# Clustered attention into a Fourier mix and an FFN on one core: scores from float16 halves for every pair, one turned head in each first-sequence pair, odd weight pieces split on GpSimd

## The chip, the cores and the metric

One core of a Trainium2 chip runs the kernel. The metric is the device time of one execution in microseconds. Three runs of the kernel before took 983.2, 986.29 and 989.46 us, the median being 986.29.

## What is computed

Four sequences of 768 tokens, 8 heads of 64 dimensions. In each head every query and key goes to the nearest of 16 centroids, and a query attends only to keys of its own cluster. The result is mixed by a two-dimensional Fourier transform (its real part), normalised, and goes through an FFN of 512 x 2048 x 512 with two residual additions.

```python
q_assign = np.argmax(np.einsum('bhsd,hcd->bhsc', q_n, c_n), axis=-1)
k_assign = np.argmax(np.einsum('bhsd,hcd->bhsc', k_n, c_n), axis=-1)
mask = q_assign[:, :, :, None] == k_assign[:, :, None, :]
scores = np.where(mask, scale * np.matmul(q, k.transpose(0, 1, 3, 2)), -1000000000.0)
attn = np.exp(scores - np.max(scores, axis=-1, keepdims=True))
attn_out = np.matmul(attn / (np.sum(attn, axis=-1, keepdims=True) + 1e-09), v)
X = np.fft.fft(np.fft.fft(x, axis=1), axis=2)          # x: the heads side by side
u = x + np.real(X)
un = (u - mean) / np.sqrt(var + 1e-06)
out = u + np.maximum(un @ w_ch1, 0.0) @ w_ch2
```

## The kernel before

Everything wants float32 accuracy. Most products are therefore made of float16 halves: a value is scaled by a power of two, split into a high half and the low rest, and three products (high by high, high by low, low by high) are summed in PSUM. Where float32 itself is used, TensorE takes the operands as they are.

Heads are worked in 16 pairs, four for each sequence; a pair's two heads lie in the two halves of the 128 partitions.

- `prep(pr)` loads q and k (`load`), takes the largest magnitudes (`largest`, VectorE), spreads them over the partitions and makes powers of two of them (`scales`), splits q and k (`split_qk`: the high half cast by ScalarE, the low one subtracted by VectorE), multiplies with the centroids, transposes the 16 cluster scores, finds the best cluster and makes one-hot rows, which a transposing DMA turns into `oht`. For pairs below `FULL`, that is 0 to 5, q and k are kept as float32: their magnitudes are not taken, they are not split, and the products with the centroids (line 441) and the scores (line 506) are float32.
- `scores(pr)` has six steps (128 queries each). A step makes the scores of both heads (line 506 or 509) and adds the cluster penalty by one-hot products (line 514); for each head VectorE then takes the row maximum (line 528) and ScalarE the exponential (line 530). For a head that is not in `TURN`, the result is cast to float16 (line 540 on GpSimd for pairs 0 to 3, line 542 on ScalarE for the others), the low half is subtracted on GpSimd (line 543), and both are transposed by a DMA on SP's queue into one of six buffers `pt`.
- `turns(pr)` does this for the heads in `TURN`: TensorE transposes the float32 result (line 562), VectorE or ScalarE copies it out of PSUM (lines 565 and 567).
- `attend(pr)` multiplies with V: 18 float16 products for a transposed head (lines 595 to 597), float32 ones for a turned head (line 590). `finish` divides by the sums (lines 605 to 609) and writes the pair's columns of X.

`Weights` loads the two FFN matrices in 32 pieces of 128 x 512 and splits each into halves: `signs` (ScalarE), `block` (a common scale), `join` (TensorE puts the float32 value into PSUM) and `halve`: ScalarE writes the high half from PSUM, VectorE the low one (lines 734 and 735). `Fourier.transform` runs when a sequence's four pairs are finished; `norms` and `layer` of `FeedForward` follow, with the up-projection at line 1064 and the down-projection at line 1106.

The order is written by hand twice over. `PLAN` is a list of words: `s0*2` means two further steps of pair 0's scores, `w` a step of the weights, `f1` one of the second sequence's FFN, and so on; it sets the order in which instructions are created. `TABLE` then permutes each engine's own list by relative jumps, and `apply` fixes the result by dependencies. Each engine works strictly in its order. Weights, transposes and loads all stand on SP's queue. The buffers around the change: one `scr` for natural q and k, two each of `hlq` and `hlk` for split ones, two of `ph` and two of `p32`, two score tiles in PSUM (`ps_big`), three of `ps_f`, one of `ps_o`.

## Time and profile before

| what | value |
|---|---|
| median of three runs | 986.29 us |
| profiled execution, its time | 981.39 us |
| its span (first to last instruction) | 979.5 us |
| TensorE busy | 924.7 us (94%) |
| VectorE busy | 560.1 us (57%) |
| ScalarE busy | 565.8 us (58%) |
| GpSimd busy | 552.7 us (56%) |
| granted TensorE clock, mean | 0.991 |

Busy time on TensorE runs to the modelled end of each matmul, so neighbours overlap, and a stretch that shows 100% has no visible gap but is not an array at its peak. How long a group really holds TensorE is read from start to start. On VectorE, too, one instruction starts a little before the end of the one ahead. A row of the table of stages gives, after the stretch, the busy microseconds and the count of instructions of each engine, the granted clock as a share of full speed, and the mean share of time that the 16 DMA engines had work (over 1 where transfers queue).

### The profile page before, as it was taken

What the parts mean: (1) busy time and instruction counts of PE and PEld (TensorE: products, weight loads), DVE (VectorE), ACT (ScalarE), POOL (GpSimd) and SP (SyncE); (2) the same over time, 40 slices, a digit from 0 to 9 for tenths busy, and PEclk for the clock granted to TensorE, in tenths of its full rate; (3) what the DMA queues carried; (4) which work ended last, traced back from release to release, by engine and by line L of the source; (5) the groups of instructions that cost most, each with busy time, mean ns of one, the idle gap of its engine ahead of it and who ended that gap; (6) DMA issues with size and microseconds to landing.
All of it is one profiled execution on the core that took longest, in us unless ns stands there. A gap on an engine that the chain in (4) does not pass through costs nothing.

```text
span 979.5 us, 23040 instructions
## 1 busy us (share of the span) xinstructions
PE 924.7 (94%) x9189; PEld 614.9 (63%) x9189; DVE 560.1 (57%) x1314; ACT 565.8 (58%) x896; POOL 552.7 (56%) x675
## 2 busy tenths in 40 slices
PE   3889999788999999999999999999999999999998
PEld 1357658465657657567757658667667585677583
DVE  5887897877556555577656664677544324611010
ACT  5667776567656756567757657368666552433140
POOL 2751640449956757559957758369857552553140
PEclk9999999898999999999999999999999999999999
DMA  9894993497877789497888777587757642311000
GB/s 345 182 236 154 228 254 79 100 186 159 150 139 128 151 148 168 78 176 166 157 174 145 128 153 158 95 168 158 129 99 135 115 76 61 66 33 33 12 12 22
DMA packets 359739, 131.18 MB, mean 134 GB/s; under 512 B 344272, under 2 KB 345296, under 8 KB 359632
## 3 DMA queue, kind: packets, MB, share of 16 engines
q1 hardware_dynamic: 359632, 129.72, 65.1%
q8 instruction: 72, 1.18, 0.5%
q14 instruction: 35, 0.29, 0.1%
HBM read 43.17 MB, written 6.29 MB: 50 GB/s over the span
## 4 chain that ended last, share of the span: by engine, by line
PE 51%; DMA 13%; POOL 6%; ACT 5%; DVE 3%; issue 3%; SPq 1%; POOLq 0%; ACTq 0%; DVEq 0%
PE ps_f L1064 21%; PE ps_f L1106 18%; DMA pt<-ph 11%; POOL ph L543 4%; PE ps_big L509 4%; ACT ph L542 2%; PE ps_o L595 2%; PE ps_f L912 1%; PE ps_o L596 1%; PE ps_o L597 1%; PE ps_big L514 1%; ACT p L530 1%; PE ps_big L506 1%; POOL arena L1073 1%; DVE ps_big L528 1%
## 5 line engine op out<-in xcount | busy, mean ns | idle before, releaser
L543 POOL TENSOR_TENSOR ph<-p,ph 128x768 f16<-128x768 f32 x144 | 240.1, 1671 | 148.5 <-ACT ph L542 141.0
L1064 PE MATMUL ps_f<-arena,w1h 128*128 128x256 f16 x1536 | 266.3, 274 | 7.2 <-DMA arena<-arena 3.3
L1106 PE MATMUL ps_f<-w2h,arena 128*128 128x512 f16 x768 | 237.5, 379 | 0.0
L1064 PE MATMUL ps_f<-arena,w1l 128*128 128x256 f16 x768 | 210.6, 274 | 0.0
L1106 PEld LDWEIGHTS <-arena 128*128 128x128 f16 x1152 | 109.5, 98 | 125.8 <-issue 2.1
L530 ACT ACTIVATE p<-ps_big,rmx 128x768 f32<-128x768 f32 x144 | 128.6, 898 | 76.6 <-DVE ps_big L528 53.0
L528 DVE TENSOR_SCALAR_CACHE_REDUCE ps_big<-ps_big,sce 128x768 f32<-128x768 f32 x120 | 118.6, 1023 | 88.6 <-PE ps_big L514 83.0
L1073 POOL TENSOR_TENSOR arena<-arena 128x256 f16<-128x256 f32 x192 | 129.1, 680 | 70.8 <-ACT arena L1072 66.8
L1064 PEld LDWEIGHTS <-w1h 128*128 128x128 f16 x1536 | 151.0, 98 | 24.9 <-DMA arena<-arena 3.4
L542 ACT CAST ph<-p 128x768 f16<-128x768 f32 x144 | 119.1, 830 | 71.4 <-DMA pt<-ph 70.3
L1106 PE MATMUL ps_f<-w2l,arena 128*128 128x512 f16 x384 | 145.5, 379 | 0.0
L595 PE MATMUL ps_o<-v,pt 128*128 128x66 f16 x1008 | 105.5, 194 | 17.5 <-DMA pt<-ph 16.1
L1072 ACT ACTIVATE arena<-ps_f,wrel 128x256 f16<-128x256 f32 x192 | 89.6, 473 | 43.4 <-DVE arena L1069 43.2
L595 PEld LDWEIGHTS <-pt 128*128 128x128 f16 x1008 | 92.2, 96 | 33.3 <-DMA pt<-ph 20.9
L1069 DVE TENSOR_SCALAR arena<-ps_f,wrel 128x256 f32<-128x256 f32 x96 | 46.2, 481 | 114.4 <-PE ps_f L1064 85.1
L596 PE MATMUL ps_o<-v,pt 128*128 128x64 f16 x1008 | 105.1, 194 | 0.0
L597 PE MATMUL ps_o<-v,pt 128*128 128x66 f16 x1008 | 104.6, 192 | 0.0
L596 PEld LDWEIGHTS <-pt 128*128 128x128 f16 x1008 | 92.9, 97 | 2.9 <-issue 0.3
L597 PEld LDWEIGHTS <-pt 128*128 128x128 f16 x1008 | 93.2, 99 | 0.0
L1064 PEld LDWEIGHTS <-w1l 128*128 128x128 f16 x768 | 75.5, 98 | 13.9 <-issue 4.5
L1071 ACT ACTIVATE arena<-ps_f,wrel 128x256 f32<-128x256 f32 x96 | 45.3, 472 | 46.3 <-PE ps_f L1064 41.3
L509 PE MATMUL ps_big<-hlk,hlq 64*128 64x384 f16 x720 | 70.7, 324 | 1.2 <-ACT p L530 1.1
(196 smaller groups left out, 1379.2 us busy)
## 6 DMA issues: line engine op xcount, KB each, us to landing
arena<-in_moe_w_ch_dram SPq DMA_DIRECT2D x32, 512.0 KB, 5.0
vst<-in_v_dram SPq DMA_DIRECT2D x16, 384.0 KB, 4.1
out_dram<-arena SPq DMA_DIRECT2D x24, 256.0 KB, 2.1
scr<-in_q_dram SPq DMA_DIRECT2D x12, 384.0 KB, 3.9
scr<-in_k_dram SPq DMA_DIRECT2D x12, 384.0 KB, 4.5
pt<-ph SPq DMA_TRANSPOSE x156, 3.9
arena<-in_cs_dram SPq DMA_DIRECT2D x12, 192.0 KB, 4.0
arena<-in_ss_dram SPq DMA_DIRECT2D x12, 192.0 KB, 3.9
```

What stands on the lines that cost most here:

```text
L509: nc.tensor.matmul(out=ps[j][:, hf, 0:SH], lhsT=hq[rows[j], a, sl], rhs=hk[rows[j], c, hs], start=(i == 0), stop=False)
L528: nc.vector.tensor_scalar(out=ju, in0=ps[j][:, :, 0:SH], scalar1=ne, scalar2=None, op0=ALU.mult, op1=ALU.min, accum_out=m)
L530: nc.scalar.activation(x, ju, AF.Exp, bias=m, scale=-1.0)
L542: nc.scalar.copy(out=ph[:, 0], in_=p32)
L543: nc.gpsimd.tensor_tensor(out=ph[:, 1], in0=p32, in1=ph[:, 0], op=ALU.subtract)
L595: nc.tensor.matmul(out=o[:, at:at + W], lhsT=hi, rhs=v16[:, kt, 0:W], start=(kt == 0), stop=False)
L596: nc.tensor.matmul(out=o[:, at:at + D], lhsT=hi, rhs=v16[:, kt, 66:130], start=False, stop=False)
L597: nc.tensor.matmul(out=o[:, at:at + W], lhsT=lo, rhs=v16[:, kt, 0:W], start=False, stop=(kt == ST - 1))
L1064: nc.tensor.matmul(out=ps.rearrange("p (t x) -> p t x", x=P), lhsT=a[:, dc, fs], rhs=c[:, :, dc], start=(i == 0), stop=(i == 11))
L1072: nc.scalar.activation(hh[:, f], ps, AF.Relu, scale=rel[:, f:f + 1])
L1073: nc.gpsimd.tensor_tensor(out=hl[:, f], in0=r, in1=hh[:, f], op=ALU.subtract)
L1106: nc.tensor.matmul(out=ps, lhsT=a[:, f, ts], rhs=c[:, f], start=(i == 0), stop=(i == 47))
```

## The change

Five edits.

1. `FULL` goes from 6 to 0: no pair keeps float32 q and k. Pairs 0 to 5 load into `scr`, take all three magnitudes, split q and k, and use the float16 paths for the centroids and the scores, as pairs 6 to 15 do already.
2. `TURN` names the second head of each of pairs 0 to 3, where it named both heads of pairs 1 and 3. There are four turned heads as before.
3. `halve` treats odd pieces in another way: ScalarE copies the scaled float32 value to SBUF, one buffer at `X32`, and GpSimd subtracts the high half. Even pieces stay as they were.
4. `load` has a condition for small `FULL` that is never true at 0.
5. `PLAN` and `TABLE` are new throughout.

```diff
-2 -3 0 1 .2 6 0 3 0 -13 12 0 -13 12 -13 12 -16 16 -15 4 10 0 -17 4 6 4 1 -17 10 6 2 -7 1 4 0 -5 0 3 8 -9 0 11 -12 .2 4 0 -6 5
+.9 4 -5 .3 3 -3 0 3 -3 0 1 5 -4 -3 0 12 27 -35 -6 0 1 0 3 -3 0 32 0 -33 0 4 -4 0 28 0 -30 4 -4 0 26 0 -28 1 0 24 0 -23 -4 0
...
-    TURN = {(1, 0), (1, 1), (3, 0), (3, 1)}
+    TURN = {(p, 1) for p in range(4)}
     EV = {(st, 0) for st in range(6)}
-    FULL = 6
+    FULL = 0
...
-        if pr < self.FULL and pr % 3:
+        if pr < self.FULL and (pr % 3 or self.FULL < 3):
...
         nc.scalar.activation(hi, ps, AF.Copy, scale=s)
-        nc.vector.scalar_tensor_tensor(out=lo, in0=ps, scalar=s, in1=hi, op0=ALU.mult, op1=ALU.subtract)
+        if k % 2:
+            x = self.arena.at(self.X32 if k < 32 - 2 * self.LATE else self.place(k), [P, DM], F32)
+            nc.scalar.activation(x, ps, AF.Copy, scale=s)
+            nc.gpsimd.tensor_tensor(out=lo, in0=x, in1=hi, op=ALU.subtract)
+        else:
+            nc.vector.scalar_tensor_tensor(out=lo, in0=ps, scalar=s, in1=hi, op0=ALU.mult, op1=ALU.subtract)
...
     PLAN = """
-w v0 p0 v1 c l*2 c p0*2 v2 p1 p2 l*2 v3 p0 v0*2 p1 l w p1 p0*4 w p1 s0*2 a0 s0*7 p1*2 s0*2 p1 a0*2 s0 p1 p3*2 w*3 l w*2 l w
+p0*2 w p0 v0 p0*5 l p1 c*2 p0*2 l*2 w p1*2 l p0*2 l v1 p1*3 p2 p1 w*2 p1 w*3 p1 l v2 w l w*3 p1 l*2 s0*2 u0 s0*2 u0 s0*2 v0
```

What this does to the engines' orders is shown at three places. Line numbers of the changed kernel are one higher up to line 735 and six higher behind line 741; `L415` there is the split that was line 414, `L529` the row maximum that was 528, `L741` the even pieces' low half, `L738` and `L739` the two new instructions of odd pieces.

The first place is VectorE, around the first row maximum of pair 0. Before, it stands behind the one-hot rows of pair 1 (`oh`) and the scale of the first weight block:

```order
L395 TENSOR_REDUCE amx<-vst 128x1
L472 TENSOR_TENSOR oh<-ac,ps_f 128x12x16
L59 TENSOR_SCALAR ps_f<-ps_f 128x1
L476 TENSOR_TENSOR oh<-ac,ps_f 128x6x16
L61 TENSOR_SCALAR winv_85<-ps_f 128x1
L476 TENSOR_TENSOR oh<-ac,ps_f 128x6x16
L63 RECIPROCAL wsc<-winv_85 128x1
L528 TENSOR_SCALAR X_64,rmx<-ps_big 128x768 x2
L735 SCALAR_TENSOR_TENSOR w1l<-ps_f,wsc,w1h 128x512
```

In the changed kernel the scales and the splits of pair 1 stand ahead of it:

```order
L633 TENSOR_SCALAR sce<-scp 128x1 x2
L415 SCALAR_TENSOR_TENSOR hlq<-scr,scp,hlq 128x768
L415 SCALAR_TENSOR_TENSOR hlk<-scr,scp,hlk 128x768
L715 TENSOR_REDUCE arena<-ps_f 128x1
L729 SCALAR_TENSOR_TENSOR ps_f<-arena,ps_f 128x512
L58 TENSOR_SCALAR ps_f<-arena 128x1
L729 SCALAR_TENSOR_TENSOR ps_f<-arena,ps_f 128x512
L59 TENSOR_SCALAR ps_f<-ps_f 128x1
L368 SCALAR_TENSOR_TENSOR v_599<-vst,scp,v_599 128x6x64
L61 TENSOR_SCALAR winv_85<-ps_f 128x1
L63 RECIPROCAL wsc<-winv_85 128x1
L529 TENSOR_SCALAR X_64,rmx<-ps_big,sce 128x768
```

Pair 0's own reductions and splits stand further up, ahead of the centroids; the row maximum now has two heads' worth of preparation ahead of it, and its scale is read from `sce`.

The second place is GpSimd, in the steps of pair 0 and 1, where `p_391`, `p_624` and the like are the second kind of buffer for transposed heads. Before, both heads of a step come together, two casts and two subtractions:

```order
L540 CAST ph<-X_64 128x768
L540 CAST p_264<-X_64 128x768
L543 TENSOR_TENSOR ph<-X_64,ph 128x768
L543 TENSOR_TENSOR p_264<-X_64,p_264 128x768
L540 CAST ph<-X_64 128x768
```

In the changed kernel one head of a step comes at a time, and subtractions of weight pieces stand between them:

```order
L541 CAST p_624<-X_64 128x768
L544 TENSOR_TENSOR p_624<-X_64,p_624 128x768
L739 TENSOR_TENSOR w1l<-arena,w1h 128x512
L541 CAST ph<-X_64 128x768
L544 TENSOR_TENSOR ph<-X_64,ph 128x768
L541 CAST p_771<-X_64 128x768
L544 TENSOR_TENSOR p_771<-X_64,p_771 128x768
L739 TENSOR_TENSOR w1l<-arena,w1h 128x512
```

So a transpose of the first sequence can have a weight piece ahead of it, which none had.

The third place is VectorE, around the last finish of pair 3 (line 609, then 610) and the fold of the Fourier step (line 851, then 857). Before, four low halves of the weights come behind that finish:

```order
L609 TENSOR_TENSOR X_63<-ps_o,rs 128x3x128
L773 TENSOR_TENSOR winv_86<-winv_86,winv_85 128x16
L735 SCALAR_TENSOR_TENSOR w2l<-ps_f,wsc,w2h 128x512 x2
L728 SCALAR_TENSOR_TENSOR ps_f<-arena,ps_f 128x512 x2
L851 TENSOR_TENSOR arena<-X_63 128x1536
L735 SCALAR_TENSOR_TENSOR w2l<-ps_f,wsc,w2h 128x512 x2
L528 TENSOR_SCALAR ps_big,rmx<-ps_big 128x2x384 x2
```

In the changed kernel the weights are through by then, and the splits of pair 5 and reductions of a later pair have their place:

```order
L610 TENSOR_TENSOR X_63<-ps_o,rs 128x3x128
L857 TENSOR_TENSOR arena<-X_63 128x1536
L415 SCALAR_TENSOR_TENSOR hlq<-scr,scp,hlq 128x768
L529 TENSOR_SCALAR ps_big,rmx<-ps_big,sce 128x2x384 x2
L415 SCALAR_TENSOR_TENSOR hlk<-scr,scp,hlk 128x768
L529 TENSOR_SCALAR ps_big,rmx<-ps_big,sce 128x2x384 x2
L841 SCALAR_TENSOR_TENSOR arena<-arena,vseq 128x768
```

What moved here is which foreign work stands between the steps of the first Fourier transform: weights before, preparation of pairs now.

## Rows read from the trace of the kernel before

**Rows 1.** Busy times by stage: stretch, each engine's microseconds (instructions), clock, DMA.
```profile
core 0: us, PE busy (x) PEld busy (x) DVE busy (x) ACT busy (x) POOL busy (x), PEclk, DMA share, GB/s
0.00:30.00 30.00, 13.00 (x55) 5.32 (x55) 17.78 (x64) 15.18 (x21) 8.26 (x45) 1.00 0.80 292
30.00:181.00 151.00, 142.68 (x1317) 94.22 (x1315) 123.19 (x290) 107.42 (x143) 66.05 (x70) 0.99 0.79 182
181.00:229.00 48.00, 35.80 (x381) 23.45 (x379) 40.52 (x96) 28.37 (x45) 30.41 (x30) 0.92 0.93 177
229.00:979.00 750.00, 733.23 (x7440) 491.92 (x7440) 378.59 (x868) 414.81 (x690) 447.96 (x533) 1.00 0.61 115
```
**Rows 2.** Timeline (start, microseconds, instruction): pair 3's last finish, the first up-projection.
```profile
180.58 0.54 DVE L609 TENSOR_TENSOR X<-ps_o,rs 128x384 f32<-128x384 f32 x1
...
229.30 0.39 PE L1064 MATMUL ps_f<-arena,w1h 128*128 128x256 f16 x1 [3.26 <-DMA arena<-arena]
```
**Rows 3.** Busy times in four stretches of the first stage, columns as in rows 1.
```profile
40.00:60.00 20.00, 17.65 (x204) 9.45 (x204) 17.90 (x47) 15.04 (x18) 17.98 (x16) 1.00 1.17 236
75.00:110.00 35.00, 35.00 (x275) 26.58 (x276) 26.40 (x59) 25.38 (x34) 9.89 (x9) 1.00 0.59 168
110.00:145.00 35.00, 32.94 (x359) 19.32 (x358) 31.86 (x80) 26.50 (x35) 21.64 (x25) 0.95 1.14 239
145.00:180.00 35.00, 35.00 (x283) 26.88 (x283) 26.66 (x64) 21.87 (x32) 2.77 (x6) 1.00 0.27 77
```
**Rows 4.** TensorE's timeline: a float32 score step, a float16 one, what follows each.
```profile
61.09 1.56 PE L506 MATMUL ps_big<-hlk,hlq 64*128 64x384 f32 x8
62.59 0.34 PE L514 MATMUL ps_big<-oht 32*128 32x384 bf16 x4
...
401.11 1.15 PE L509 MATMUL ps_big<-hlk,hlq 64*128 64x384 f16 x12
402.19 0.34 PE L514 MATMUL ps_big<-oht 32*128 32x384 bf16 x4
```
**Rows 5.** TensorE's groups by line: count, busy microseconds, mean ns; idle before.
```profile
L446 PE MATMUL ps_f<-hlq,ct 128*32 128x384 f16 x60 | 6.7, 329 | 0.2 <-ACT arena L1072 0.2
...
L441 PE MATMUL ps_f<-hlq,arena 128*32 128x384 f32 x16 | 4.0, 585 | 0.0
```
**Rows 6.** VectorE's groups by line and shape, whole span.
```profile
L395 DVE TENSOR_REDUCE amx<-scr 128x1 f32<-128x768 f32 x20 | 18.8, 946 | 8.8 <-DMA scr<-in_q_dram 8.8
...
L414 DVE SCALAR_TENSOR_TENSOR hlq<-scr,scp,hlq 128x768 f16<-128x768 f32 x10 | 15.2, 1522 | 0.8 <-ACT hlq L413 0.8
...
L735 DVE SCALAR_TENSOR_TENSOR w1l<-ps_f,wsc,w1h 128x512 f16<-128x512 f32 x16 | 11.7, 747 | 1.9 <-ACT w1h L734 1.9
...
L414 DVE SCALAR_TENSOR_TENSOR hlk<-scr,scp,hlk 128x768 f16<-128x768 f32 x10 | 11.0, 1097 | 0.0
...
L405 DVE TENSOR_REDUCE ps_f<-ps_f 128x3 f32<-128x384 f32 x10 | 5.6, 560 | 2.6 <-PE ps_f L48 2.5
...
L405 DVE TENSOR_REDUCE ps_f<-ps_f 128x1 f32<-128x128 f32 x6 | 1.8, 296 | 1.7 <-PE ps_f L48 1.7
```
**Rows 7.** A split of q: shortest, median, longest of ten; one behind a subtraction.
```profile
L414 DVE SCALAR_TENSOR_TENSOR hlq<-scr,scp,hlq x10: 1012/1336/2394, 228.9 to 698.5; 128x768 f16<-128x768 f32 x10
...
322.98 1.65 POOL L543 TENSOR_TENSOR ph<-p,ph 128x768 f16<-128x768 f32 x1
...
323.35 2.09 DVE L414 SCALAR_TENSOR_TENSOR hlq<-scr,scp,hlq 128x768 f16<-128x768 f32 x1
```
**Rows 8.** Groups by line on ScalarE and GpSimd that the added instructions resemble.
```profile
L734 ACT ACTIVATE w1h<-ps_f,wsc 128x512 f16<-128x512 f32 x16 | 10.6, 680 | 8.4 <-DVE wsc L63 8.0 <-DVE ps_f L728 0.3
...
L413 ACT ACTIVATE hlq<-scr,scp 128x768 f16<-128x768 f32 x10 | 9.3, 928 | 5.0 <-DVE scp L630 2.5 <-PE ps_big L506 1.4 <-PE ps_big L509 1.1
...
L1034 POOL TENSOR_TENSOR arena<-arena 128x512 f16<-128x512 f32 x20 | 24.4, 1219 | 8.4 <-ACT arena L1033 8.3
```
**Rows 9.** Busy times in a stretch with a lowered clock, columns as in rows 1.
```profile
185.00:196.00 11.00, 8.09 (x66) 5.23 (x66) 11.00 (x17) 5.16 (x7) 6.43 (x3) 0.69 0.60 126
```

More of the change, by code (lines that the diff above doesn't have):

```diff
@@ L153 @@
[L153 to L156 removed]
+.28 11 3 -16 1 -2 18 2 -21 1 0 -3 7 -6 6 -7 0 3 -4 5 .3 1 0 1 .2 1 0 -3 15 0 -14 0 -3 3 0 -3 4 0 -3 -2 4 0 -3 6 -3 2 .2 48 0
@@ L157 @@
+-26 -9 .3 11 18 2 -3 -29 28 67 -67 -12 11 -30 2 33 -37 -3 2 1 1 1 71 .3 1 -79 1 0 1 -2 1 24 45 30 -102 0 14 -15 1 14 -15 0 65
+4 -71 0 93 .2 -88 88 -89 13 -12 11 -14 1 56 18 0 -3 -73 79 1 -82 51 -52 .2 9 0 -11 10 -11 10 0 -10 9 0 -11 10 -11 10 1 -13 10
+1 -13 12 .6 52 -53 .5 44 -28 -18 17 -18 17 0 -12 11 -12 11 .2 -14 13 -14 13 .5 15 -16 3 8 5 .3 1 -2 1 -8 -3 0 8 0 12 .2 17
+-18 17 -24 -11 0 9 -10 0 12 0 25 -40 13 25 -40 39 -40 0 39 -40 39 0 -41 40 1 -34 .5 26 1 -8 -22 .6 2 .8 11 0 14 -15 .13
 """,
@@ new lines @@
+0 1 -9 8 1 -5 49 0 -49 44 0 -45 .3 -26 2 22 1 .3 1 5 -6 .2 25 -26 -6 5 1 0 10 -10 0 -18 27 7 -19 0 6 -7 .4 4 2 -3 0 -17 11 5
+0 2 4 .3 7 -8 0 11 -12 0 1 23 -26 1 1 .3 2 7 -11 2 10 -11 .2 8 -9 5 -6 7 -8 8 0 1 -2 7 -7 .3 45 -43 0 41 -41 36 0 -38 -8 0 6
+0 -25 0 23 0 13 -12 -3 13 -14 3 1 0 7 -8 0 -8 0 -12 41 -25 3 -4 4 .2 5 -6 0 5 -22 44 -30 0 4 .2 5 7 -8 .6 1 6 -7 0 -24 1 43
+-23 0 38 -29 -11 2 .2 5 -6 5 -6 6 -2 -6 0 7 0 -4 3 1 .4 49 -49 1 .2 2 0 -8 44 0 1 -61 9 15 -11 0 2 0 5 -5 0 30 -31 2 .2 25
@@ L166 @@
+-26 9 -10 .8 1 18 -19 .3 15 -16 .7 8 .9 1 0 -3 2 0 2 -3 2 -3 2 .3
 """,
@@ new lines @@
+p10 t1 v12 s9*4 p10 f0 p10 f0 s9*2 p10 f1*3 s9*2 f1 f0 p10 f1*2 p12*2 t1 p11 p10 p11 a8*5 p11 a8 p10*2 t1 p13 s10*3 f1*6 s10
+f1*3 p11 v9*2 a9*2 f1 v11*2 s10 a9*3 p12 a8 f1 a9 f1 s10 n1 f1 v10 n1 a9*8 n1 p11 f1 n1 s10*6 p12 n1 f1 p11 v10 f1 p14 f1
+p11*2 f1 p12 f1 p14 p12 p11 p12 f1 p12 f1*4 a10 v12 p12 a10*3 p11 s11 a10*6 f1 a10*2 s11*2 f1 t2 v13 a10 a11 p12 a10 a11 s11
+a11*2 f1 p12 s11*3 f1 s11 a11*4 s11 f1 s11*2 p12 s11 f1 a11 s12*3 a11*2 s12*2 a11 f1*6 p13*4 f1 a11 f1 p13 s12*7 a11 f1*4
+p13*3 f1*2 p13 a12 f1*6 v12 f1*6 a12 f1*2 a12 p13 f1*2 p13 f1 p14 t2 a12 t2 f1 s13 f1 t2*2 a12 p15 t2 a12 v13 a12*2 p14 a12*4
@@ new lines @@
+v13 t2*7 v14 a12 s13 t2 p14 t2*2 a12 f1 t2*3 f1 t2*2 p15 p14*2 s13 f1 s13 t2 s13 v14 s13*2 a13*4 t2*2 s13 n2 f2 s13 f2*4 s13
+f2*2 v15 f2*2 p15 p14 p15 v14 p14 f2*4 a13*2 f2 n2 a13*2 s13 f2 p14 a13 s13 a13 p14 p15*2 f2 a13 f2 a13 p14 n2 f2 a13 f2*2
+s14*4 a14 s14 a13 f2*3 s14*2 a14 v15*2 s14*5 p15 f2*6 p15 f2 p15 f2 a14*2 f2 a14 f2*2 p15*2 f2 a14*9 f2 p15 f2*7 s15 a15
+s15*7 n2 s15*4 a15*5 n2 a15*8 t3 f2*24 t3 n2 f2*2 t3*14 f2*2 t3*3 f2 t3 n3*2 t3*2 f3*10 n3*2 f3*21 t3 f3*9 t3 f3*2 n3 f3 n3
+f3*29
```

162 lines of the change are left out of this document (72 added, 90 removed).

## The prediction

> **What bounds the kernel now.** I read the page first, then the busy times by stage, then the timeline around the places the change touches. The program falls into three stages [rows 1]: until 181 us the attention of the first sequence (pairs 0 to 3) beside the conversion of the FFN weights; from 181 to 229 us the Fourier step and the first norm; from 229 us on the FFN with the other sequences beside it. The last finish of pair 3 on VectorE begins at 180.58 us and the first up-projection at 229.30 us [rows 2]. In the third stage TensorE is busy 733.2 of 750 us: what it no longer has to do there comes off the end, and so does whatever moves the 229 us.
>
> The first stage is not TensorE's alone. It alternates [rows 3]. Where a pair has both heads turned by TensorE (75 to 110 us, 145 to 180 us) TensorE is busy 35.0 of 35.0 us, VectorE 26.4 and 26.7, and the DMA share is 0.59 and 0.27. Where a pair has none (40 to 60, 110 to 145) VectorE is busy 17.9 of 20 and 31.9 of 35, nine tenths, the DMA share is 1.17 and 1.14, and TensorE has gaps. So two engines set the pace in turn, and VectorE shows in these rows how densely it can be packed: 0.90. Over the whole of 30 to 181 us it is busy 123.2 of 151, that is 0.82 [rows 1].
>
> **TensorE's work.** A score step of pairs 0 to 5 is 8 float32 records, 1.50 us from its start to that of the one-hot products behind it (61.09 to 62.59); with float16 halves it is 12 records in 1.08 us (401.11 to 402.19) [rows 4]. Six steps in six pairs: 36 x 0.42 = 15.1 us less. The cluster products: one side's float32 rows take 4.0 us in four pairs, the float16 ones 6.7 us in ten [rows 5], so 0.33 x 6 = 2.0 us less. The scales of these pairs take three small products instead of one, 12 more, some tenths of a microsecond each at most, and I take 1 us more. Together 16 us less. The turned heads stay four, so transposes, evictions and float32 products only change their place, and the transposes through DMA stay 24 in the first sequence.
>
> Of these 16 us most lie ahead of 229 us: of the 36 float32 steps 31 stand in TensorE's order ahead of the first up-projection, 5 behind it. In the changed order 32 of the 36 stand ahead. The stage behind 229 us so loses 5 x 1.50 - 4 x 1.08 = 3.2 us, and TensorE being full there, **3 us come off the end**. What the other 13 us bring depends on who sets the 229 us.
>
> **VectorE's work in the first stage**, counted in the two orders up to the second finish of pair 3, with durations from [rows 6]:
> - 9 more reductions for the scales of q and k, 0.946 each: +8.5 us.
> - 10 more splits of q and k (two of pair 5 come later): 5 x (1.522 + 1.097) = +13.1 us.
> - six reductions over three columns instead of one, 0.560 against 0.296: +1.6 us. Twelve one-column multiplies for the score's scale: between nothing and 0.3 each; I take 1.8 us.
> - the low halves of the odd weight pieces leave: 16 subtractions instead of 28 stand ahead of this point, 12 x 0.747 = -9.0 us.
>
> Sum +16 us. Bounds: with splits at their shortest (1.01) and the multiplies at nothing 11 us; with all ten splits at the longest that the rows show for one (2.39) [rows 7] and the multiplies at 3.6, 28.6 us. Nothing below the lower bound is possible, as the reductions and splits are instructions that were not there. VectorE was busy 141.0 us until 181 [rows 1]; it will need about 157, between 152 and 170.
>
> **ScalarE and GpSimd.** ScalarE gets 12 casts of q and k at 0.93 and 16 copies of odd pieces at 0.68 [rows 8]: 22 us on top of the 122.6 us that it is busy until 181 [rows 1], 80% of the time: covered, as long as the stage is not shorter than some 160 us. GpSimd gets 16 subtractions of 128x512. It has no such one of a weight piece before; the nearest row is that of the norm, 1.22 us with the same shapes [rows 8]: 20 us on 74.3 until 181, covered too. What is queued behind them are its casts and subtractions for the next transposes; in the order shown they stand one at a time between those, so a transpose is late by 1.2 us, not more. If that cover went, each would delay a product, and TensorE waits for it.
>
> **The start.** The first softmax of pair 0 stands on VectorE behind the scales and the four splits of pairs 0 and 1: four reductions and four splits, 4 x 0.946 + 2 x 2.62 = 9 us, in a stretch of which VectorE leaves 12 of 30 us idle [rows 1]. I take half of it as hidden: the first scores come some 4 us later, with pair 1 already prepared, and VectorE has then done 22 us of its work at 30 us instead of 17.8. On SP's queue q and k of pair 0 are now first, ahead of V and the weights; their number stays.
>
> **Sum.** The stage ends where VectorE is through: 157 - 22 = 135 us at the 0.90 that rows 3 show it holding, 150 us from 30 us on, so at 180 us instead of 181. TensorE then needs less than its 155.7 us and has room. From there to 229 us VectorE is busy 40.5 of 48 us [rows 1]; three reductions and two splits come in (5.5 us), four weight subtractions leave (3.0 us): the 7.5 us idle hide that; uncovered it would be 2.5. So 1 us, and 3 us behind 229: 4 us less. The profiled execution took 981.4 us with a span of 979.5; the median of the three runs is 986.3, and the sum goes onto that: **982 us**. The likeliest case by itself reaches from 974 (VectorE packed at 0.95) to 990 (0.85).
>
> **Rivals.**
> (1) TensorE still sets the first stage. For it speaks that the four stretches of [rows 3] are full in turn, two on TensorE and two on DMA and VectorE, and that one turned and one transposed head in each pair spreads both loads evenly. VectorE would have to hold 135 us in 138, 0.98, against it. But if the splits cost 1.01 and the start hides all nine microseconds, it is 152 - 27 = 125 us in 138, 0.91, just what it has shown. Then all 16 us come off: 970 us.
> (2) Slower: GpSimd holds VectorE up. A split of q takes 1.01 us at its shortest and 2.39 at its longest; the one at 323.35 us begins while GpSimd's subtraction of 322.98 (1.65 us) runs, and takes 2.09 [rows 7]. The change puts ten such splits and at least 16 GpSimd instructions into the same stage. At 2.39 each VectorE needs 170 us: 148 at 0.90 is 164 us from 30 us on, an end at 194, 13 us late. TensorE, idle for longer, would also lose clock: between 185 and 196 us its granted clock is 0.69, a stretch at the lower of its two levels (1.2 instead of 2.4 GHz) after it had waited, and costs (1 - 0.69) x 11 = 3.4 us [rows 9]. One more of these: 986 + 13 + 3 - 3 = 999 us. From an end of the stage at 194 us on, the kernel is slower by more than 1%. Against it: the splits' mean of 1.3 us already holds such meetings, at a GpSimd that is busier in the third stage (448 of 750) than in the first (66 of 151).
> The Trainium skill, "SBUF — State Buffer", section "SBUF: two separate sides", gives a reason: VectorE and GpSimd share a pair of ports that is locked for a whole instruction, and a VectorE instruction with two SBUF inputs, as the split is, blocks against a GpSimd one that reads SBUF. By that rule, the trace agrees (2.09 us behind a running subtraction against 1.01 alone); by that rule alone moving subtractions from VectorE, where one input is in PSUM, to GpSimd while adding splits is the wrong way round, and would end at the 999 us of this rival.
>
> **Chances.** VectorE-paced with nothing gained or lost in the stage 0.45; TensorE-paced 0.31; VectorE held up or packed badly by the new order 0.24. About 1% is what a measurement of this kernel can tell from no change: 976.4 to 996.2 us. Faster by more: rival 1 and a little of the first case's lower end, 0.33. Slower by more: most of rival 2, 0.22. Within: 0.45. Range: from below rival 1 (967, when the waits on DMA of the two stretches without turned heads go too) to rival 2 (1000).
>
> **What would show it.** The second finish of pair 3 (180.6 us before) and the first up-projection (229.3): at 180 and 228 in my case, near 169 and 216 in rival 1, at 194 and beyond 240 in rival 2. VectorE's share in 34 to 180 us near 0.90, and TensorE's below the 142.7 of 151. A score step of pair 0 at 1.1 us. The splits' mean near 1.3 us; at 2 us rival 2 holds. Behind the first up-projection the rest should take 747 us; if it takes more than 755, the new order of the third stage, which I took as equal to the old one, is what failed.

## The result, and the profile after

The change made the kernel slower. Its median is 996.08 us over nine runs (990.41 to 998.85), against 985.45 us for the kernel before in nine runs beside them: ratio 1.0102, with a 95% interval of 1.0084 to 1.0120. Forecast were 982 us and a gain of 4. The profiled execution of the changed kernel has a span of 991.1 us, 11.6 more than before.

In the changed kernel's code line numbers are one higher than before as far as line 735, six higher behind 741. Its busy times by stage (stretch, each engine's microseconds with instructions, clock, DMA), cut where its own stages end, answer to [rows 1]:

```profile
core 0: us, PE busy (x) PEld busy (x) DVE busy (x) ACT busy (x) POOL busy (x), PEclk, DMA share, GB/s
0.00:30.00 30.00, 8.85 (x38) 3.95 (x38) 18.92 (x60) 17.07 (x23) 6.57 (x42) 1.00 0.69 243
30.00:183.40 153.40, 135.02 (x1435) 93.03 (x1454) 139.07 (x318) 121.27 (x165) 87.14 (x88) 0.98 0.79 188
183.40:239.60 56.20, 36.71 (x471) 24.29 (x471) 46.77 (x99) 35.71 (x54) 36.96 (x36) 0.88 0.87 173
239.60:991.10 751.50, 729.04 (x7408) 489.39 (x7408) 373.54 (x860) 409.33 (x685) 444.36 (x527) 1.00 0.61 114
```

The second stage of the kernel before, cut in the same way, beside it:

```profile
180.60:229.30 48.70, 36.20 (x383) 23.45 (x379) 41.22 (x97) 28.98 (x45) 31.11 (x30) 0.92 0.92 176
```

The two marks of [rows 2], on VectorE's and TensorE's timeline after:

```profile
183.42 0.55 DVE L610 TENSOR_TENSOR X<-ps_o,rs 128x384 f32<-128x384 f32 x1
```
```profile
239.58 0.28 PE L1070 MATMUL ps_f<-arena,w1h 128*128 128x256 f16 x1 [2.13 <-DMA arena<-arena]
```

So the first stage ends 2.8 us later than before, the second takes 56.2 us instead of 48.7 (7.5 more), the third 751.5 instead of 750.2. TensorE is busy 909.6 us instead of 924.7: the 15 us that were to leave it did leave it, and it waits for 27 us more. In the third stage, too, where 3 us were to come off, its busy time falls by 4.2 us and its waits grow by 5.5 (17.0 to 22.5), so that nothing comes off.

The longest stall stands at the start of the second stage. VectorE's timeline there:

```profile
184.00 1.91 DVE L857 TENSOR_TENSOR arena<-X 128x1536 f32<-128x1536 f32 x1
185.84 5.95 DVE L415 SCALAR_TENSOR_TENSOR hlq<-scr,scp,hlq 128x768 f16<-128x768 f32 x1
191.71 1.01 DVE L529 TENSOR_SCALAR_CACHE_REDUCE ps_big<-ps_big,sce 128x768 f32<-128x768 f32 x1
```

and GpSimd's in the same microseconds:

```profile
184.26 2.23 POOL L869 TENSOR_TENSOR arena<-arena,X 1x255 f32<-1x255 f32 x1
186.46 1.63 POOL L544 TENSOR_TENSOR ph<-p,ph 128x768 f16<-128x768 f32 x1
188.06 1.15 POOL L739 TENSOR_TENSOR w2l<-arena,w2h 128x512 f16<-128x512 f32 x1
189.18 1.79 POOL L858 TENSOR_TENSOR arena<-arena 128x765 f32<-128x765 f32 x1
```

One split of q (pair 5, L415) takes 5.95 us; the sixteen of them in the kernel:

```profile
L415 DVE SCALAR_TENSOR_TENSOR hlq<-scr,scp,hlq x16: 1007/1019/5948, 12.8 to 708.7; 128x768 f16<-128x768 f32 x16
```

(shortest, median, longest). GpSimd runs four instructions without a pause from 184.26 to 190.97 us, one of them (L739) new: VectorE's order has no weight piece left behind the finish, but GpSimd's still has this one. The split is through 0.8 us after the run. The row maxima of pair 4 (L529) stand behind it. What TensorE waits for from 181 to 240 us:

```profile
PE ps_big L510 <- ACT p L531: 8.5, 6, 4.6
PE ps_o L596 <- DMA pt<-ph: 5.1, 2, 3.2
PE ps_f L918 <- DMA arena<-arena: 2.3, 2, 1.4
PE ps_f L1070 <- DMA arena<-arena: 2.1, 1, 2.1
```

The first line, waiting for pair 4's exponentials, was 1.1 us in that stretch before:

```profile
PE ps_big L506 <- ACT p L530: 1.1, 2, 0.7
```

The split that holds up their row maxima was my first suspect.

### The profile page after: what moved, and what is told of

The parts are those of the page before. It is cut to its first block, busy times and chain, and to the rows that moved or that the text cites. A ratio compares the mean times of both kernels' runs of the same rounds, so it can differ in the third digit from the quotient of the medians.

```text
span 991.1 us, 23402 instructions
## 1 busy us (share of the span) xinstructions
PE 909.6 (92%) x9350; PEld 610.7 (62%) x9369; DVE 578.3 (58%) x1334; ACT 583.4 (59%) x924; POOL 575.0 (58%) x691
## 4 chain that ended last, share of the span: by engine, by line
PE 45%; DMA 18%; POOL 9%; DVE 8%; ACT 7%; issue 4%; SPq 1%; another core or an unknown queue 0%; POOLq 0%; ACTq 0%; DVEq 0%
PE ps_f L1112 18%; PE ps_f L1070 15%; DMA pt<-ph 14%; POOL ph L544 6%; PE ps_big L510 4%; ACT ph L543 3%; PE ps_f L918 2%; DMA arena<-arena 2%; DVE X L529 1%; ACT p L531 1%; PE ps_o L596 1%; DVE ps_big L529 1%; PE ps_big L515 1%; DVE amx L396 1%; PE ps_o L597 1%
## 5 line engine op out<-in xcount | busy, mean ns | idle before, releaser
L529 DVE TENSOR_SCALAR_CACHE_REDUCE ps_big<-ps_big,sce 128x768 f32<-128x768 f32 x144 | 142.0, 1021 | 77.9 <-PE ps_big L515 66.5
L1079 POOL TENSOR_TENSOR arena<-arena 128x256 f16<-128x256 f32 x192 | 132.4, 696 | 78.4 <-ACT arena L1078 73.9
L510 PE MATMUL ps_big<-hlk,hlq 64*128 64x384 f16 x1152 | 117.0, 328 | 12.6 <-ACT p L531 9.5
L1075 DVE TENSOR_SCALAR arena<-ps_f,wrel 128x256 f32<-128x256 f32 x96 | 46.2, 481 | 119.9 <-PE ps_f L1070 86.7
L510 PEld LDWEIGHTS <-hlq 64*128 64x128 f16 x1152 | 51.2, 95 | 62.9 <-issue 35.1
```

The source lines that it names most:

```text
L510: nc.tensor.matmul(out=ps[j][:, hf, 0:SH], lhsT=hq[rows[j], a, sl], rhs=hk[rows[j], c, hs], start=(i == 0), stop=False)
L529: nc.vector.tensor_scalar(out=ju, in0=ps[j][:, :, 0:SH], scalar1=ne, scalar2=None, op0=ALU.mult, op1=ALU.min, accum_out=m)
L1079: nc.gpsimd.tensor_tensor(out=hl[:, f], in0=r, in1=hh[:, f], op=ALU.subtract)
```

## The experiments

All were timed against the kernel before on the same chip. The table has them in the order of this section; marks and busy times are those of each profiled execution, and the second stage is the time between the two marks.

A mark comes from one execution, and executions differ. The changed kernel and the seven of the table that share its first stage (split later, fold first, weight piece later, Fourier first and mended, relief of stage two, relief with Fourier first) have their second finish between 181.1 and 185.1 us. "Before, six reductions more" shares its first and its third stage with the kernel before: the second finish is 182.2 against 180.6, the third stage 754.4 against 750.2. The lower clock differs from execution to execution, too (last column but one). So a difference of some 2 us in the first stage, or 4 in the third, need not mean anything; the ratios, from 4 to 10 runs of each kernel, carry more.

| kernel | ratio (95%) | second finish | first up-projection | second stage | granted clock in it | VectorE busy in it |
|---|---|---|---|---|---|---|
| before | 1 | 180.6 | 229.3 | 48.7 | 0.92 | 41.2 |
| changed | 1.0102 (1.0084 to 1.0120) | 183.4 | 239.6 | 56.2 | 0.88 | 46.8 |
| split later | 1.0130 (1.0106 to 1.0155) | 183.6 | 241.4 | 57.8 | 0.80 | 50.2 |
| fold first | 1.0103 (1.0078 to 1.0128) | 182.7 | 238.4 | 55.7 | 0.82 | 47.3 |
| weight piece later | one run: 1000.0 us | 183.2 | 242.9 | 59.7 | 0.86 | 46.8 |
| VectorE's low halves | 1.0112 (1.0070 to 1.0155) | 185.7 | 242.2 | 56.5 | 0.91 | 46.2 |
| narrow maxima | 1.0092 (1.0056 to 1.0129) | 181.0 | 237.8 | 56.8 | 0.79 | 45.8 |
| float32 scores | 1.0045 (1.0026 to 1.0064) | 186.2 | 241.6 | 55.4 | 0.85 | 39.8 |
| half prepared | 1.0090 (1.0061 to 1.0119) | 185.6 | 246.0 | 60.4 | 0.87 | 49.8 |
| Fourier first | 1.0150 (1.0121 to 1.0179) | 183.4 | 247.5 | 64.1 | 0.81 | 45.3 |
| Fourier first, mended | 1.0074 (1.0050 to 1.0098) | 181.1 | 237.6 | 56.5 | 0.88 | 44.8 |
| float32, Fourier first | 1.0108 (1.0073 to 1.0142) | 183.9 | 243.4 | 59.5 | 0.84 | 43.6 |
| before, six reductions more | 1.0033 (1.0005 to 1.0061) | 182.2 | 235.7 | 53.5 | 0.83 | 47.8 |
| relief of stage two | 1.0060 (1.0038 to 1.0083) | 183.9 | 237.2 | 53.3 | 0.84 | 39.0 |
| relief, Fourier first | 1.0047 (1.0022 to 1.0073) | 185.1 | 240.8 | 55.7 | 0.85 | 39.3 |
| relief of both stages | 1.0052 (1.0025 to 1.0079) | 181.7 | 237.9 | 56.2 | 0.88 | 39.4 |

### Is it the held split? Three small moves

Moves are made on the decoded order (from place, to place).

```
+    MOVES = {"DVE": ((329, 331),)}                                   # split later
+    MOVES = {"DVE": ((329, 331), (335, 331)), "Pool": ((126, 124),),
+             "Activation": ((193, 189),)}                            # fold first
+    MOVES = {"Pool": ((125, 128),)}                                  # weight piece later
             for a, b in self.MOVES.get(e, ()):
+                order.insert(b, order.pop(a))
```

> The changed kernel with one VectorE instruction moved: the split of q of pair 5, which takes 5.95 us at 185.84 us there, stands behind the two row-maximum passes of pair 4 that waited behind it. Theory A (the split is held by GpSimd's back-to-back run of four instructions, and what stands behind it on VectorE carries the loss on to the Fourier step): the two passes begin at about 186 instead of 191.7 us, ScalarE's high half of the fold near 191 instead of 196.2, the first up-projection at 234 to 236 instead of 239.6, and the kernel takes 4 to 5 us less than the changed one, 1.005 to 1.006 of the kernel before. Theory B (VectorE is simply fuller there, and the split only shows it): what stood behind the split is late for other reasons, the first up-projection stays within 1 us of 239.6, ratio 1.009 to 1.011.

> As the run with the split moved, and the chain of the Fourier step's first transposed fold is put ahead of other work on each engine: GpSimd's fold ahead of the second cast's subtraction and of the weight piece, ScalarE's high half ahead of four instructions of pair 4's softmax, VectorE's low half ahead of the two splits. Theory A: the high half begins near 188.5 us as in the kernel before (188.0), the low half near 189.5, the first up-projection at 230 to 233 us, ratio 1.001 to 1.003. Theory B: the fold comes early but the first up-projection moves by less than 3 us, ratio 1.007 to 1.010, because the work put back is late then. A third outcome, with TensorE short of softmax work instead: the first up-projection near 236, ratio 1.005 to 1.007.

> The changed kernel with one GpSimd instruction moved: the subtraction of weight piece 88's turn (1.15 us at 188.06 us), which stands between two instructions of the run that goes on while VectorE's split of q of pair 5 takes 5.95 us, comes two casts later. If the split is held as long as GpSimd runs back to back, it takes 4.7 to 4.9 us; if it is slow for a reason of its own (its operands, a transfer), it stays at 5.8 to 6.1 us.

That GpSimd holds the split was confirmed: with the weight piece (1.15 us) taken out of GpSimd's run, the split takes 4.83 us, 1.12 less.

```profile
185.66 4.83 DVE L419 SCALAR_TENSOR_TENSOR hlq<-scr,scp,hlq 128x768 f16<-128x768 f32 x1
```

That its place ahead of the row maxima costs the kernel its time was refuted. With the split behind them those run at 185.98 us, but the second stage is no shorter, and the ratios of both moves (1.0130 and 1.0103) are no better than the changed kernel's. The split itself is held there, too, for 5.67 us. With the fold put first as well, two instructions take the split's place as the ones held:

```profile
188.54 2.53 DVE L845 SCALAR_TENSOR_TENSOR arena<-arena,vseq 128x768 f16<-128x768 f32 x1 [1.41 <-ACT arena L844]
191.00 2.39 DVE L419 SCALAR_TENSOR_TENSOR hlq<-scr,scp,hlq 128x768 f16<-128x768 f32 x1
```

and the fold, through at 191.07, is transposed only when SP's queue gets to it at 200.27, behind the loads of pair 6, which wait until the split of k (to 194.32) has freed their buffer. The third move shows the same queue from another side: SP's timeline of "weight piece later".

```profile
187.94 1.43 SPq L550 DMA_TRANSPOSE pt<-ph  x1
197.92 0.33 SPq L903 DMA_DIRECT2D arena<-in_ny_dram  x1
198.35 0.38 SPq L396 DMA_DIRECT2D scr<-in_q_dram  x1
198.78 0.42 SPq L396 DMA_DIRECT2D scr<-in_k_dram  x1
199.31 5.30 SPq L550 DMA_TRANSPOSE pt<-ph  x2
204.70 1.46 SPq L868 DMA_TRANSPOSE arena<-arena  x1
```

The load of a Fourier table (in_ny) goes into bytes of the arena that the new subtraction still reads, so it waited until GpSimd had done it at 197.9 us, and everything queued behind it too.

### Which engine sets the first stage?

```
-        if k % 2:
-            ...
-        else:
-            nc.vector.scalar_tensor_tensor(out=lo, ...)
+        nc.vector.scalar_tensor_tensor(out=lo, ...)                  # VectorE's low halves
```
```
+        if pr < 6 and i < 2:
+            x = x[:, 0:64]                                           # narrow maxima, in largest()
```
```
-    FULL = 0
+    FULL = 6                              # float32 scores, with VectorE's low halves too
```

> The changed kernel with the low halves of the odd weight pieces made by VectorE again (16 subtractions of 0.75 us each come back to VectorE, 16 copies leave ScalarE and 16 subtractions of 1.16 us leave GpSimd), each put where ScalarE's copy stood. If VectorE sets the first stage at the 0.90 that the prediction took, 12 of the 16 make it 12 x 0.75 / 0.90 = 10 us longer: second finish of pair 3 near 193, ratio 1.018 to 1.021. If GpSimd's subtractions cost VectorE more by holding its splits than they relieve it of, the ratio falls to 1.000 to 1.006 and the split of q of pair 5 takes under 5 us. If another engine sets the stage, the second finish stays within 2 us of 183.4 and the ratio within 0.003 of 1.010.

> The changed kernel with the twelve added reductions for the scales of q and k of pairs 0 to 5 over 64 of the 768 columns (the scales come from a part of the values; 0.95 us of VectorE each become about 0.15, so some 9.5 us of VectorE's work leave, 3 to 4 of them ahead of the first softmax); no instruction changes its place. If VectorE's load sets the pace of the first stage: first softmax at 30 us instead of 33.1, second finish of pair 3 at 173 to 175 instead of 183.4, ratio 1.000 to 1.003. If VectorE has room (10 us more work on it moved the second finish by 2.3 us only in the run with the low halves back on it): the gain is that of the start alone, second finish at 179 to 181, ratio 1.006 to 1.008.

> Two of the three edits undone with the new order and the new turned heads kept: the scores and cluster products of pairs 0 to 5 in float32 again (no split, no reduction of q and k for them), low halves of the odd weight pieces on VectorE. TensorE gets back some 16 us of work, VectorE loses about 24 and gets 9 back. If the preparation of the halves is what ate the gain, TensorE's waits ahead of 229 us fall by the 16 us that it works more and the time is that of the changed kernel or less: ratio 1.003 to 1.010. If the new order or the four turned heads at their new places cost by themselves, TensorE keeps its waits and the 16 us come on top: ratio 1.018 to 1.027.

The first 30 us and the rest of the first stage, for VectorE's low halves, narrow maxima and float32 scores in turn (the columns are those of the first table; DVE's busy time, which is VectorE's, and PE's, which is TensorE's, are to be added over the two rows of a kernel):

```profile
0.00:30.00 30.00, 8.04 (x34) 3.69 (x35) 18.16 (x59) 16.27 (x22) 6.59 (x42) 1.00 0.70 243
30.00:185.70 155.70, 137.41 (x1439) 93.03 (x1457) 147.23 (x334) 115.01 (x152) 70.42 (x73) 0.99 0.78 185
```
```profile
0.00:30.00 30.00, 8.87 (x40) 4.02 (x42) 16.07 (x60) 17.12 (x23) 6.56 (x42) 1.00 0.70 243
30.00:181.00 151.00, 134.17 (x1435) 92.08 (x1454) 133.43 (x318) 120.84 (x165) 87.08 (x88) 0.98 0.79 191
```
```profile
0.00:30.00 30.00, 9.89 (x34) 4.20 (x36) 13.18 (x53) 15.04 (x20) 6.57 (x42) 1.00 0.78 268
30.00:186.20 156.20, 144.94 (x1311) 97.48 (x1326) 129.64 (x307) 107.42 (x142) 68.91 (x73) 0.98 0.79 179
```

VectorE has 165.4, 149.5 and 142.8 us to do ahead of the second finish, and the changed kernel 158.0; the finish comes at 185.7, 181.0, 186.2 and 183.4. So 7.4 us more on VectorE came with an end 2.3 later, 8.5 us less with one 2.4 earlier, and 15 us less, with 11 more on TensorE (154.8 instead of 143.9), with one 2.8 later. If VectorE set the stage, the first two would have ended near 193 and at 173 to 175. Neither engine sets the stage by itself; what a microsecond of either is worth there cannot be read from moves that are hardly larger than the scatter of the mark. Nor can the ratios of the first two (1.0112 and 1.0092) be told from the changed kernel's: splitting odd pieces on GpSimd by itself brings and costs nothing that shows.

The float32 run says more. By then TensorE (154.8) and VectorE (142.8) have what they have in the kernel before (155.3 and 140.6, by the same cuts), and yet its second finish comes 5.6 us later (3.3 in "float32, Fourier first", which shares its first stage), its first up-projection 12.3 us later, and by all its runs it is 0.45% slower. Only the new order and the new places of the turned heads are left in it; no run parts the two. They cost 4.4 us by themselves (2.6 to 6.3), where I had put nothing. The order was made for the halves, so that it costs the same with them is an inference.

The other part of the loss is the halves' own. The changed kernel takes 5.6 us more than the float32 one (3.0 to 8.2 from the two intervals), although TensorE has less to do in it. Up to the first up-projection TensorE waits for 59.0 us in the changed kernel (239.6 less 180.6 busy) and for 41.7 in the float32 one (241.6 less 199.9), whose second stage has this row:

```profile
186.20:241.60 55.40, 45.04 (x438) 28.00 (x437) 39.77 (x97) 33.30 (x51) 35.13 (x35) 0.85 0.91 177
```

Its ratio lies in the first of the two ranges that were expected, that of a preparation which eats the gain.

### Does order make the second stage long?

Blocks of the order are rearranged on all five engines, so that both folds, their halves and transposes and the first Fourier products stand ahead of pair 4's third and fourth score steps. The core of the first try:

```
+    PLACES = {
+        "PE": ((180, [180, 181, 182, 183, 187, 188, 184, 190, 191, 185, 186, 189]),),
+        "DVE": ((328, [328, 330, 331, 335, 337, 329, 332, 341, ...]),),
+        "Activation": ((189, [193, 189, 190, 191, 192, 201, ...]),),
+        "Pool": ((124, [126, 124, 127, 133, 128, 125, ...]),),
+        "SP": ((86, [86, 91, 89, 87, 88, 90, 95, ...]),),
             for at, to in self.PLACES.get(e, ()):
+                order[at:at + len(to)] = [order[i] for i in to]
```

> The changed kernel with the Fourier step's start put ahead of pair 4's softmax on all five engines between 184 and 215 us: on TensorE its first two products ahead of the product of the second score step and of the fourth score step, on VectorE, ScalarE and GpSimd both folds and their halves ahead of pair 4's third and fourth step, on SP the transposes of the folds ahead of the loads of pair 6, which wait there until VectorE has split q and k of pair 5. With the fold alone put first the first product still came at 204.4 us, behind two more rounds of pair 4 than in the kernel before (193.9). Theory C (the order of the second stage: the Fourier chain stands behind pair 4's softmax on TensorE and behind pair 6's loads on SP): first product at 194 to 197 us, first up-projection at 228 to 233, ratio 1.000 to 1.004, as what is put off finds room in the third stage. Theory B (the stage is full of work, whatever its order): first up-projection at 236 or later, ratio 1.008 to 1.011. Between them: the first up-projection comes at 228 to 233, but the softmax work put off is missed in the third stage, whose length grows by what the second lost: ratio 1.007 to 1.010.

> The changed kernel with the Fourier step ahead of pair 4's softmax, mended: the first try held SP's queue until 199 us, because the load of a Fourier table waits for GpSimd's subtraction of the last weight piece, which I had moved back; here that subtraction stays early, the transpose of the first fold is issued ahead of pair 6's loads, and GpSimd's long addition for the fold's middle row is moved back instead. Theory C (the second stage is as long as its order makes it: the Fourier chain queued behind pair 4's softmax and behind SP's loads): first Fourier product at 195 to 198 us instead of 204.8, first up-projection at 229 to 234 instead of 239.6, ratio 1.000 to 1.005. Theory B (the stage is simply fuller): the first product comes early, but the first up-projection not before 236, ratio 1.008 or more. If the softmax work put off is missed later: first up-projection at 229 to 234, ratio 1.007 to 1.010.

> The kernel with the new order and turned heads but float32 scores (1.0045 of the kernel before), with the Fourier step put first in its second stage as well. That stage takes 55.4 us there, as long as in the changed kernel (56.2) and 6.7 more than before (48.7), though VectorE has no split of pair 5 and 18 us less to do by then. Theory C: the order alone makes it long; first up-projection at 232 to 236 instead of 241.6, and since TensorE is full behind it, ratio 0.995 to 1.000, level with the kernel before. Theory B: no earlier than 239, ratio 1.003 to 1.006.

The first try fell to my own move: with the weight piece's subtraction late again, in_ny was issued at 199.06 us and the fold's transpose, whose operands were ready at 190.68, behind it at 199.49. Mended, the first Fourier product came 11 us earlier than in the changed kernel (204.8), ahead even of the kernel before (193.89):

```profile
193.52 1.90 PE L928 MATMUL ps_f<-arena 128*128 128x257 f16 x12
```

and still the stage took 56.5 us. TensorE's waits in it, 181 to 238 us, had only moved:

```profile
PE ps_o L606 <- DMA pt<-ph: 7.0, 3, 4.2
PE ps_f L890 <- DVE arena L851: 3.9, 1, 3.9
PE ps_big L520 <- ACT p L541: 2.9, 4, 0.9
```

Its time is 2.8 us less than the changed kernel's by the ratios, give or take 3.0, which cannot be told from nothing. In the float32 kernel the same rearrangement made the stage longer (59.5) and the kernel slower (1.0108 against 1.0045). So theory C, in the form in which I could test it, fell: these orders are not shown to be better than the change's own.

### Does VectorE's added work make it long?

Half prepared is the float32 kernel with `FULL = 3` in place of 6. Six reductions are added to the kernel before, and the work that the changed kernel has more in its second stage is left out:

```
-                self.largest(pr, m, i)
+                for _ in range(3 if pr == 6 else 1):                 # before, six reductions more
+                    self.largest(pr, m, i)
```
```
+        if pr == 6:
+            x = x[:, 0:64]                                           # relief, in largest()
...
+        if pr == 5:
+            nc.vector.memset(hl[:, 1], 0.0)                          # relief, in split_qk()
+        else:
             nc.vector.scalar_tensor_tensor(out=hl[:, 1], ...)
```

> The changed kernel with VectorE's low halves (1.011) and float32 scores for pairs 0 to 2 only: pairs 3 to 5 keep the float16 halves. It stands halfway between that kernel and the one with float32 scores in all six pairs (1.0045). If the preparation costs where it stands in the crowded first 110 us (pairs 0 to 2), the time is that of the float32 kernel less the 8 us of TensorE that pairs 3 to 5 save: first softmax at 31 us, ratio 0.998 to 1.003. If each pair's preparation costs what it costs anywhere, the time lies between the two: ratio 1.006 to 1.009. If pairs 3 to 5 are the dear ones (their splits meet the fold): 1.010 or more.

> The kernel before, unchanged but for VectorE work in its second stage: the three reductions for pair 6's scales are made three times, and the six added ones (0.95 us each, one input in SBUF, 5.7 us together) stand between 184 and 204 us at the places where the changed kernel has its splits and reductions. This is the step of the prediction by itself: it took that 7.5 us of VectorE's idle time in 181 to 229 us would hide 5.5 us. If they hide it: first up-projection within 1 us of 229.3, ratio 0.999 to 1.001. If VectorE's share of that stage cannot rise above the 0.87 that it has in the kernel before and in the changed one alike: the stage is 5.7 / 0.87 = 6.5 us longer, first up-projection at 235 to 236, ratio 1.005 to 1.007.

> The changed kernel with the work that VectorE has more of in the second stage left out, every instruction at its place: pair 5's low halves of q and k are filled with zeros instead of computed (that part of the result is left out; the two splits, 5.95 and 1.01 us there, become two fills that read nothing, and SP's loads of pair 6 no longer wait for them), and the three reductions of pair 6 read 64 columns (2.8 us become about 0.4). Some 9 us of VectorE leave the stage, 4.9 of them the time that GpSimd held one split. If VectorE's load makes the stage 56.2 instead of 48.7 us (six reductions added to the kernel before made it 4.8 us longer): the stage falls to 48 to 51 us, first up-projection at 231 to 234, ratio 1.002 to 1.005. If the new order makes it long whatever VectorE has to do (55.4 us with float32 scores): it stays at 54 or more, first up-projection at 237 or later, ratio 1.007 to 1.010.

All three point one way, none as far as it might have. The kernel before with 5.7 us more on VectorE has a second stage 4.8 us longer in its profiled execution:

```profile
182.20:235.70 53.50, 39.36 (x383) 25.49 (x379) 47.80 (x104) 29.79 (x46) 32.37 (x30) 0.83 0.86 160
```

and takes 3.3 us more by all runs (0.5 to 6.0), between the two outcomes expected; its first up-projection came where the second outcome had it. (The share of 0.87 in the expectation is in no row: VectorE was busy 0.85 of the stage in the kernel before and 0.83 in the changed one.) The profiled execution, 991.96 us, is among the three longest of its ten (983.03 to 992.04), so its 4.8 us are more than the usual cost; and most of them are not waits. TensorE has as many records there as before, 383, and is busy 3.2 us longer, as more of them fall to the lower level of its clock. Its stretches at that level, in this kernel (two rows) and in the kernel before:

```profile
186.50:200.20 13.70, 9.60 (x63) 6.16 (x64) 13.70 (x18) 4.86 (x6) 7.74 (x4) 0.50 0.62 125
203.60:207.00 3.40, 3.40 (x14) 1.64 (x14) 2.05 (x5) 2.40 (x5) 2.38 (x2) 0.50 0.77 141
```
```profile
187.30:194.10 6.80, 5.47 (x32) 3.08 (x33) 6.80 (x12) 3.97 (x5) 3.40 (x3) 0.50 0.47 90
```

Whether the added work brought that or the execution, one trace cannot say. The changed kernel with its added work left out has a stage 2.9 us shorter:

```profile
183.90:237.20 53.30, 39.23 (x471) 25.52 (x471) 38.96 (x99) 35.79 (x54) 36.09 (x36) 0.84 1.01 183
```

and takes 4.1 us less (1.0060 against 1.0102; 1.3 to 7 from the two intervals), again between the two outcomes expected. The fills also let SP load pair 6 earlier, so that not all of this need be VectorE's time. And of the 0.67% between the float32 run and VectorE's low halves, 0.45 are there when pairs 3 to 5 alone are prepared (1.0 to 7.8 us; from there to all six pairs, the intervals tell nothing). The last of them falls into the second stage: there a split of q takes 4.17 us, held once more, and the stage is the second longest of all. How much of this comes from the second stage the run does not show.

> The changed kernel with both changes to the second stage at once: VectorE's added work left out (pair 5's low halves filled with zeros, pair 6's reductions over 64 columns; 56.2 to 53.3 us by itself) and the Fourier chain ahead of pair 4's softmax on all five engines (56.5 by itself, with the first Fourier product at 193.5 instead of 204.8 us). If load and order hide each other: stage 48 to 50 us, first up-projection at 230 to 233, ratio 0.999 to 1.003. If the order has no share: stage 53 us, ratio 1.005 to 1.007.

> As the run with both changes to the second stage, and the twelve added reductions of pairs 0 to 5 over 64 columns too: some 18 us of VectorE's work fewer than in the changed kernel, TensorE's work unchanged. The reductions alone moved the second finish from 183.4 to 181.0 and the time by 0.1%. If VectorE's load costs in both stages: second finish near 181, first up-projection at 228 to 231, ratio 0.996 to 1.000: then the halves' gain on TensorE is there once VectorE has room. If the first stage is set by the new order: second finish 181 or later, ratio as without the reductions, 0.999 to 1.003.

With load and order both changed the stage is 55.7 and 56.2 us, and the ratios 1.0047 and 1.0052 cannot be told from the relief alone. What makes up the rest of the stage's 7.5 us is thus not settled. One part can be read from the clock. The stretches at the lower level in the second stage, in the changed kernel, and in the one with relief and Fourier first:

```profile
185.90:199.60 13.70, 5.75 (x59) 2.98 (x60) 10.15 (x10) 6.68 (x10) 8.43 (x8) 0.50 0.63 142
```
```profile
187.90:198.10 10.20, 6.76 (x67) 3.73 (x68) 6.29 (x12) 7.30 (x11) 8.23 (x5) 0.50 0.73 140
204.90:211.70 6.80, 6.21 (x68) 4.48 (x68) 5.08 (x13) 3.81 (x8) 1.93 (x2) 0.50 1.10 176
```

TensorE is busy for 5.75 us at half speed in the first, for 12.97 in the second. At full speed this would take about half, so that the price, an estimate, is 2.9 and 6.5 us; in the kernel before it is 2.7 (5.47 us busy), with six reductions more 6.5. What the relief freed was used up in part by work done at the lower clock. The clock falls while TensorE waits: at 185.9 in a wait from 184.8 to 188.0 us in the changed kernel, at 187.9 in one from 186.5 to 190.5 and at 204.9 at the end of one of 4.1 us in the other.

No run has the counterpart of the six reductions, with instructions that read two operands from SBUF; whether those would cost more is open.

## Why the prediction was wrong, step by step

- **TensorE's work: right.** 16 us less were forecast, 15.1 measured (924.7 to 909.6). A score step of pair 0 has its 12 records from 47.60 us on and its one-hot products at 48.67: 1.07 us, against 1.1 forecast. In the third stage it is busy 4.2 us less (3.2 forecast).
- **VectorE's work ahead of the second finish: right in size.** 157 us forecast, 158.0 measured, and a share of 139.07 in 153.4, 0.907 (0.90 forecast). The splits' mean is 1.39 us over 32 (1.3 taken), with the 5.95 in it. ScalarE's copies take 0.688 us and GpSimd's subtractions 1.16 and 1.21 (0.68 and 1.22 taken).
- **VectorE sets the first stage: refuted, though the number came near, by luck.** The stage ended at 183.4 (180 forecast) with the forecast share, but 7 to 15 us of VectorE's work put on or taken off moved the end by 2 to 3 us. Rival 1 fell with it: its end near 169 did not come, and TensorE's 11 us less brought 2.8 at most.
- **The start: right in its delay, not in VectorE's lead.** 4 us were forecast, the first softmax came at 33.1 instead of 29.4. But VectorE had done 18.9 us of its work at 30 us, not 22; the 139 left instead of 135 are, in the sum's own terms, what put the end at 183.4. Eight and a half microseconds of reductions taken out gave back nothing of the delay (33.04) and no time that the intervals show.
- **The second stage hides what comes in: wrong.** Forecast were 2.5 us more on VectorE, hidden in 7.5 us of idle time. VectorE had 5.6 us more (46.77 against 41.22): what the sum lacked is the hold of one split, some 4.9 us. And it was not hidden: idle time there is waiting, in the changed kernel for TensorE (4.6 us), ScalarE (3.1) and GpSimd (1.3) in turn, as they wait for VectorE. The reductions added to the kernel before show it without any of the change: 5.7 us of work cost 3.3 us of time (0.5 to 6.0). The relief puts this step at about 4 us (1.3 to 7).
- **The turned heads and the new order: taken at nothing, measured at 4.4 us** in the float32 kernel. I wrote that transposes, evictions and products only change their place. In the float32 run's execution it failed ahead of the first up-projection, in the first stage by 5.6 us and in the second by 6.7, while the third was no longer (748.9 us). The new order asks for more of TensorE in the second stage: one score step more (7 sets of one-hot products against 6), the cluster products of one pair, and 216 records of products with V against 180. Which of these costs what is open.
- **3 us off the end: did not come.** TensorE's busy time behind the first up-projection fell as forecast, its waits grew by more, and the stage took 751.5 us where 747 were forecast. The sign that I had named, beyond 755, did not show; over all kernels of the table with the new order the stage takes 747.2 to 755.3 us, and two executions with the same third stage, 750.2 and 754.4, differ by more than the term. So no run shows the 3 us: that what TensorE no longer does comes off the end, as it is nearly full there, did not hold.
- **The miss as a whole** is 14 us: 4 less were forecast, 10 more measured. The order and the turned heads are 4.4 of them. The halves with their preparation and the weight pieces, forecast at 4 us less, measured at 5.6 more, are the other 10; the step of the second stage is in these. Where the rest of these 10 arises, no run shows.
- **Rival 2: its mechanism was there, at one place.** GpSimd's holds were priced over ten splits in the first stage; there they added little (the stage ended at 183.4, not 194). The one that stands out met the Fourier step's start. The Trainium skill, "SBUF — State Buffer", section "SBUF: two separate sides", has the lock last for a whole instruction; had the split come next after the one that ran as it began, to 186.5 us, it would have ended near 187.5 (an estimate, with the 1.0 us that it takes alone). The trace shows it through at 191.79, after three more. That this rival's 999 us lie close to the 996 measured is luck: its path, an end of the first stage at 194, was not taken.
- **The range** (967 to 1000) held the time; the likeliest case's own, to 990, did not.

## What to carry to other kernels

An engine that is idle for a sixth of a stage need not have room: where the idle time is made of short waits in a chain that goes through four engines, added work can cost time (here 5.7 us of it cost 3.3), and time taken from one engine by putting work on another need not come back. A reordering is an edit with a price: undo everything else and time the order by itself before the other edits are judged. One profiled execution shows where a stage's time goes, but not whether 2 us of it are there in the next one: let the runs' times decide. And before a dependency is moved, look at what shares its queue: one load that waits for a late subtraction held a transpose behind it for nine microseconds.
